# Attention and leaky-ReLU MLP on one core: the first two batches' values over 128 partitions, and a new order of the first loads

## The chip, the cores and the metric

The kernel runs on one core of one Trainium2 chip. The metric is the device time of one execution in microseconds (us), as the median of three runs. A lower time is better.

## The reference

The program is an attention over windows, followed by a two-layer MLP on its output. There are 8 batches, 8 heads, 576 rows and 64 columns per head; all inputs and the output are fp32.

```
scores = scale * np.matmul(q, k.transpose(0, 1, 3, 2))
rel = pos[:, None] - pos[None, :]
mask_plain = (rel >= 0) & (rel < 32)                         # heads 0 to 3
mask_dil = (rel >= 0) & (rel < 128) & (rel % 4 == 0)         # heads 4 to 7
attn = softmax of scores under the head's mask
attn_out = np.matmul(attn, v)
x = attn_out.transpose(0, 2, 1, 3).reshape(4608, 512)
h = x @ w_in                                                 # 512 x 2048
g = np.maximum(0.01 * h, h)
out = g @ w_out                                              # 2048 x 512
```

## The kernel before

**Visits.** Every batch is done in four visits of two heads each, in the order `VISITS = (2, 3, 0, 1)` (L434): first the two pairs of dilated heads ("group 1"), then the two pairs of plain heads ("group 0"). A pair's q and k, transposed, and its values lie in one of six slots of the tile `slots`; within a slot the keys begin at column `KB` and the values at `VB`.

**Batches 0 and 1** (`EARLY = 2`) use a form with 128 key rows of a head pair, of which the two heads own the even and the odd partitions. `unit` does half a visit: the scores on TensorE (L944), a bias of the mask added by a matmul (L941), the exponential on ScalarE (L951), the sums (L962) and the values (L956) on TensorE, logarithm and exponential on ScalarE for the reciprocal (L972, L974), and the normalised product on VectorE into the transposed activations `xt` (L985). `rest_unit` does the last 64 rows of all heads (the exponential of the reciprocal at L1055). In the scores' matmul both heads' keys stand in one operand: those of one head in 64 partitions at every second column, those of the other in the other 64 partitions at the columns between, and what is left must be zero. So the key part of every slot is cleared once (L550), and so are the two staging tiles `vst` of the values, since a load fills only every second partition there.

**The way in.** `load` (L529) issues a DMA, all of them on SP's queue but the first keys and the first constants (ScalarE's queue). q and k land in `stg` tiles, are cast to fp16 into `nat` (L544 on ScalarE, L545 on VectorE and GpSimd), are transposed on TensorE for batches 0 to 2 (`turn`, L808) and copied out of PSUM into the slot (L556 ScalarE, L557 VectorE). Key copies of batches 0 and 1 write every second column, one copy per head. For batches 3 and later VectorE transposes (L780, L787). `load_v` (L658) brings the values into `vst` and casts them into the slot. For batches 0 and 1 it issues ten DMAs of 64 partitions, every second one, and makes two casts of 128x576 per visit; for later batches it issues four DMAs per batch over 128 contiguous partitions (of pieces of 1 KB for the dilated heads, 256 bytes for the plain heads and the last rows), and casts them in parts of 64 partitions.

**Weights** come in 16 pieces, w0 to w15: w0 to w7 are `w_in` (piece n has the rows of visit `VISITS[n % 4]` and the columns of half n // 4), w8 to w15 are `w_out`. A piece lands in a tile that is free at the time (`gt`, `wst`, parts of `xt`) and is cast to fp16.

**Batches 2 to 7** use `burst`, which does one visit in quadrants of 64x64 (scores at L1146, exponential L1245, mask L1252, the reciprocal at L1204 and L1211, the product at L1228), and is set between the matmuls of the MLP.

**The MLP** goes over 12 chunks of 384 tokens. `up` and `up_pair` multiply by `w_in` (L1275, L1309) and apply the leaky ReLU on ScalarE while leaving PSUM (L1291); the chunk's result is a tile `gt`. Chunks 8 to 11 use a scheme of seven products for eight blocks (`ups7`: L1408 the products, L1420, L1427 and L1431 what is put together). `down` (L1488) and, in seven products, `group` (L1577, sums at L1563) multiply by `w_out`; the output is stored through `osb`.

**What sets the order.** All work is given as tasks with costs to a list scheduler (`_Plan`, L212), which passes forward and backward over it, and writes an order for each engine. The word list `FIRST` (L36) gives the order of the first loads: q, k, v and r (the last 64 rows of q and k) with the batch's digit and then the group's (v01 are the values of batch 0, group 1), w with the piece's number, c the rest of the constants. Two tables correct the plan by task number: `NUDGE` (L38) shifts a priority, `HAND` (L151) fixes an engine. Constants tune it: `SERVE` multiplies the planner's time for a load after the first ones, and `PLACE + PACE * k` (L1755) is the up step of which burst k stands ahead. Before the first up matmul TensorE runs idle matmuls on zeros (L1691, L1851).

## Time and profile before

| | |
|---|---|
| median of 3 runs | 297.22 us (296.24 to 298.74) |
| the profiled execution | 297.45 us |
| its span in the profile | 295.4 us |
| TensorE (PE) busy | 283.2 us, 96% of the span |
| VectorE (DVE) busy | 230.7 us, 78% |
| ScalarE (ACT) busy | 212.5 us, 72% |
| GpSimd (POOL) busy | 79.4 us, 27% |
| moved by DMA | 47.04 MB in 140235 packets |

The profile shows one execution. The time between the span and the execution's own time, 2.05 us, lies around the first and the last instruction. The times of instructions are counted from the start of the span. A row of a time list gives start and length in us, the engine, the line of the kernel, the operation with what it writes and reads, its size, and in brackets the idle time of the engine ahead of it with what ended it. A row of a group gives the busy time and the mean length in ns of one instruction, then the idle time ahead of them. PEld is TensorE's loading of weights, which runs beside its matmuls; SPq is SyncE's queue, on which the DMAs are issued.

### The profile page before, as it was taken

What the parts mean: (1) busy time and instruction counts of PE and PEld (TensorE: products, weight loads), DVE (VectorE), ACT (ScalarE), POOL (GpSimd) and SP (SyncE); (2) the same over time, 40 slices, a digit from 0 to 9 for tenths busy, and PEclk for the clock granted to TensorE, in tenths of its full rate; (3) what the DMA queues carried; (4) which work ended last, traced back from release to release, by engine and by line L of the source; (5) the groups of instructions that cost most, each with busy time, mean ns of one, the idle gap of its engine ahead of it and who ended that gap; (6) DMA issues with size and microseconds to landing.
All of it is one profiled execution on the core that took longest, in us unless ns stands there. A gap on an engine that the chain in (4) does not pass through costs nothing.

```text
span 295.4 us, 9622 instructions
## 1 busy us (share of the span) xinstructions
PE 283.2 (96%) x3981; PEld 221.2 (75%) x3981; DVE 230.7 (78%) x451; ACT 212.5 (72%) x438; POOL 79.4 (27%) x132
## 2 busy tenths in 40 slices
PE   6779999999999989999899999999999999999995
PEld 2556767687666867776567776777899999999984
DVE  6676686985999879865769678997878889678582
ACT  4976888399798986997977888666536776665721
POOL 4333242221671754454454461000000000000000
PEclk9999999999999999999999999999999999999999
DMA  7899998979799999998999991012202110121213
GB/s 248 237 301 403 340 351 292 357 160 171 143 216 227 154 225 191 202 176 195 170 220 196 168 252 40 0 40 73 73 0 74 37 38 2 36 73 38 71 69 111
DMA packets 140235, 47.04 MB, mean 159 GB/s; under 512 B 118944, under 2 KB 137632, under 8 KB 140192
## 3 DMA queue, kind: packets, MB, share of 16 engines
q1 hardware_dynamic: 139504, 45.81, 61.9%
q8 instruction: 31, 0.51, 0.7%
q10 hardware_dynamic: 688, 0.63, 0.6%
q14 instruction: 12, 0.10, 0.1%
HBM read 36.99 MB, written 9.44 MB: 157 GB/s over the span
## 4 chain that ended last, share of the span: by engine, by line
PE 68%; DMA 12%; ACT 7%; DVE 5%; SPq 4%; issue 2%; POOL 1%; ACTq 0%; DVEq 0%; POOLq 0%
PE psum L1577 27%; PE psum L1275 14%; PE psum L1408 13%; PE psum L1488 5%; SPq L529 4%; PE psum L1309 4%; PE psum L1146 3%; DMA gt<-in_moe_w_in_dram 3%; ACT gt L1291 2%; DMA out_dram<-osb 2%; DMA con<-consts 2%; DMA vst<-in_v_dram 2%; ACT slots L556 1%; DMA stg<-in_k_dram 1%; DMA stg<-in_q_dram 1%
## 5 line engine op out<-in xcount | busy, mean ns | idle before, releaser
L1275 PE MATMUL psum<-xt,w_in 128*128 128x384 f16 x448 | 86.0, 326 | 3.3 <-ACT gt L1291 2.1
L1577 PEld LDWEIGHTS <-gt 128*128 128x128 f16 x768 | 74.3, 98 | 12.1 <-DVE gt L1563 0.2
L1577 PE MATMUL psum<-w_out,gt 128*128 128x256 f16 x512 | 64.2, 273 | 0.0
L1291 ACT ACTIVATE gt<-psum 128x384 f16<-128x384 f32 x112 | 53.2, 494 | 14.3 <-PE psum L1275 13.3
L1275 PEld LDWEIGHTS <-w_in 128*128 128x128 f16 x448 | 41.8, 98 | 27.0 <-issue 4.2
L545 POOL CAST nat<-stg 128x576 f16<-128x576 f32 (+1 forms) x42 | 30.8, 754 | 47.0 <-DMA stg<-in_k_dram 17.1
L545 POOL CAST slots<-vst 64x256 f16<-64x256 f32 (+2 forms) x58 | 29.2, 520 | 31.0 <-DMA vst<-in_v_dram 20.6
L1427 DVE TENSOR_TENSOR vst<-psum,vst 128x384 f32<-128x384 f32 x48 | 25.8, 553 | 7.4 <-PE psum L1408 6.4
L1431 ACT ACTIVATE gt<-vst 128x384 f16<-128x384 f32 (+1 forms) x32 | 21.3, 683 | 11.1 <-DVE vst L1427 11.0
L1228 DVE TENSOR_TENSOR xt<-psum,rc 128x448 f16<-128x448 f32 (+2 forms) x53 | 20.4, 424 | 7.8 <-ACT rc L1211 6.6
L544 ACT CAST slots<-vst 64x448 f16<-64x448 f32 (+3 forms) x43 | 20.3, 482 | 3.3 <-DMA vst<-in_v_dram 2.6
L1606 ACT COPY stg<-psum 128x512 f32<-128x512 f32 (+1 forms) x22 | 11.8, 538 | 15.1 <-PE psum L1577 14.9
L1245 ACT ACTIVATE ee<-psum 128x896 f16<-128x896 f32 (+3 forms) x31 | 21.5, 707 | 1.4 <-PE psum L1146 1.4
L1408 PEld LDWEIGHTS <-w_in 128*128 128x128 f16 x256 | 21.9, 98 | 0.4
L1252 DVE TENSOR_TENSOR ee<-ee,con 128x768 f16<-128x768 f16 (+1 forms) x24 | 17.0, 707 | 6.4 <-ACT ee L1245 6.2
L557 DVE COPY slots<-psum 128x512 f16<-128x512 f16 (+3 forms) x33 | 15.4, 484 | 7.4 <-PE psum L808 5.6
L1408 PE MATMUL psum<-xt,w_in 128*128 128x192 f16 x192 | 21.1, 246 | 0.0
L1420 ACT COPY vst<-psum 128x384 f32<-128x384 f32 x32 | 15.0, 475 | 6.9 <-PE psum L1408 5.7
L787 DVE STREAM_TRANSPOSE slots<-nat 128x576 f16<-128x576 f16 (+2 forms) x30 | 15.9, 556 | 3.3 <-POOL nat L545 3.2
L1204 ACT ACTIVATE rc<-psum 128x576 f32<-128x576 f32 x24 | 15.6, 651 | 2.6 <-PE psum L1146 2.2
L1408 PEld LDWEIGHTS <-stg 128*128 128x128 f16 x192 | 16.7, 98 | 0.5
L780 DVE STREAM_TRANSPOSE slots<-nat 128x576 f16<-128x576 f16 x20 | 14.5, 757 | 2.9 <-POOL nat L545 2.8
(105 smaller groups left out, 483.3 us busy)
## 6 DMA issues: line engine op xcount, KB each, us to landing
out_dram<-osb SPq DMA_DIRECT2D x32, 256.0 KB, 2.5
stg<-in_q_dram SPq DMA_DIRECT2D x40, 144.0 KB, 4.0
stg<-in_k_dram SPq DMA_DIRECT2D x40, 144.0 KB, 3.5
vst<-in_v_dram SPq DMA_DIRECT2D x12, 288.0 KB, 5.1
gt<-in_moe_w_in_dram SPq DMA_DIRECT2D x6, 512.0 KB, 8.9
vst<-in_v_dram SPq DMA_DIRECT2D x6, 512.0 KB, 4.9
stg<-in_q_dram SPq DMA_DIRECT2D x5, 512.0 KB, 7.0
stg<-in_k_dram SPq DMA_DIRECT2D x5, 512.0 KB, 7.9
```

The lines of the kernel that those rows point to most:

```text
L544: return nc.scalar.copy(out=dst, in_=src)
L545: return ENG[e].tensor_copy(out=dst, in_=src)
L787: return add("DVE", dur, [c_qk[o]] + old, lambda e: nc.vector.transpose(slot(tn, dst, 0, 128, [1, n1 - n0]), na[:, o * S + n0:o * S + n1]) ...
L1228: lambda e, args=args: nc.vector.tensor_tensor(out=args[0], in0=args[1], in1=args[2], op=ALU.mult), prio)
L1245: lambda e, p=p, np=np, part=part: nc.scalar.activation(out=at(et, 0, 128, 448 * p, [448, np], [1, n]), in_=part, func=AF.Exp, scale=SCALE ...
L1252: lambda e: nc.vector.tensor_tensor(out=at(et, 0, 128, 0, [448, 2], [1, n]), in0=at(et, 0, 128, 0, [448, 2], [1, n]), in1=at(con, 0, 128, ...
L1275: nc.tensor.matmul(ht[:, 0:n], at(w_in, 0, 128, vi * DFF + j // 2 * 256 + j % 2, [2, 128]), at(xt[m % 2], 0, 128, vi * 1152 + x0 + x, [1, n]),
L1291: lambda e: nc.scalar.activation(out=gt[c % NG][:, j * n_c + x:j * n_c + x + n], in_=ht[:, 0:n], func=AF.Prelu, alpha=0.01),
L1408: nc.tensor.matmul(bk[:, n * i:n * i + n], w(v, 2 * z + i), x(v), start=first and i == 0 and v == 0, stop=i == 1 and v == 1, skip_group_ch ...
L1427: return add("DVE", 0.08 + 2 * n * 0.00104, deps, lambda e: nc.vector.tensor_tensor(out=dst, in0=over(bk), in1=dst, op=ALU.add), begin + w ...
L1431: t = add("ACT", dur, deps + gt_free.get(c - NG, []), lambda e: nc.scalar.activation(out=dst, in_=src, func=AF.Prelu, alpha=0.01), begin + ...
L1577: nc.tensor.matmul(bk[:, x:x + HN], tl[:, off + j * step:off + j * step + 128], rhs(j), start=first and x == 0 and j == 0, stop=j == HJ - ...
```

## The change

**Values of batches 0 and 1.** They are loaded as those of the later batches are: 128 contiguous partitions, four DMAs per batch instead of ten. The two heads of a pair now own the lower and the upper 64 partitions and no longer the even and the odd ones. With that go the bias and the pair table of the constants, and the key copies, which now write contiguous columns. A batch's values are cast by 20 instructions on 64 partitions (of 256, 64, 320 and 256 columns) where eight of 128x576 did it; for half of them the plan may choose GpSimd, VectorE or ScalarE, for the other half, which move data between the partition halves, VectorE or ScalarE.

**Clears.** The four clears of `vst` (128x1152 fp32) are gone; the value part of each slot is now cleared as well as the key part (12 clears of 128x576 instead of 6).

**Table load.** ScalarE loads its activation table ahead of its first computing instruction and not ahead of its first DMA issues.

**Plan.** w7 is loaded ahead of the first values, w0 ahead of w1, w9 ahead of q10, and the order of the last weights is new. `SERVE` goes from 1.0 to 1.1, `PLACE` from 21.0 to 20.5, `PACE` from 4.25 to 4.6. The planner counts 0.5 us for the issue of a DMA that doesn't lie on 64 partitions (0.65 before). `NUDGE` and `HAND` are replaced whole; `HAND` has some 190 entries now, 11 before.

**Counts.** The compiled rows go from 451 to 445 on VectorE, from 440 to 453 on ScalarE, from 132 to 149 on GpSimd and from 199 to 187 on SP. GpSimd has 8 more casts of q and k, 3 more of the last rows and 7 more of weights; VectorE has 7 fewer of q and k. Of the value casts of batches 0 and 1 VectorE has 16 with 256 or 320 columns and three with 64, ScalarE ten and three. TensorE's matmuls are the same, with two more idle ones.

```diff
-ROOM, LATE, LANDS, SERVE, FSERVE = 256, 1.06, 0.6, 1.0, 1.04
+ROOM = 256
+LATE = 1.06
+LANDS = 0.6
+SERVE = 1.1
+FSERVE = 1.04
...
-PLACE = 21.0
-PACE = 4.25
+PLACE = 20.5
+PACE = 4.6
...
-FIRST = ('q01 q00 r0 v01 v00 w1 w0 w7 w2 w6 w3 w4 q11 w5 q10 v11 w9 w8 '
-         'w10 w13 w11 r1 v10 w12 w14 w15 c ')
+FIRST = ('q01 q00 r0 w7 v01 v00 w0 w1 w2 w6 w3 w4 q11 w5 w9 q10 v11 w10 '
+         'w8 w13 w11 r1 v10 w15 w12 w14 c ')
 NUDGE = {
-    0: 8.35, 2: 2.35, 3: -23.12, 8: -0.87, 9: -27.76, 10: -0.24, 25: -101.0, 30: -2.6, 33: 0.12, 36:
...
+    0: 87.72, 2: -74.14, 3: 109.34, 4: -121.33, 5: -62.38, 6: 44.63, 7: 83.91, 8: -101.47, 9: 29.63,
...
 HAND = {
-    61: "POOL", 338: "DVE", 454: "DVE", 459: "DVE", 763: "ACT", 764: "ACT", 1013: "ACT", 1389:
...
+    3: "DVE", 4: "DVE", 5: "DVE", 6: "DVE", 8: "DVE", 11: "DVE", 12: "DVE", 13: "DVE", 26: "DVE",
...
-TURN_AT = ('st01t', 'sssft')
+TURN_AT = ('fgfgt', 't0tft')
...
-    key = np.arange(128)[:, None] // 2
+    key = np.arange(128)[:, None] % 64
...
-    pairs = np.arange(128)[:, None] % 2 == np.arange(128)[None, :] // 64
+    pairs = np.arange(128)[:, None] // 64 == np.arange(128)[None, :] // 64
...
-        t = plan.dma(queue, 0.65, (took(n, size) * FSERVE if prio < -1400 else took(n, size, True) * SERVE), deps,
+        t = plan.dma(queue, 0.65 if dst.ap[0][1] == 64 else 0.5, (took(n, size) * FSERVE if prio < -1400 else took(n, size, True) * SERVE), deps,
...
-                               prio + 0.01 * i, deps) for x in (KB,)]
+                               prio + 0.01 * i + 0.001 * x / VB, deps) for x in (KB, VB)]
...
-    t_blank = [[clear((("DVE", 1.24), ("POOL", 1.4)), x[:, VH * hh:VH * hh + VH], None, 0.0, -2001)
-                for hh in range(2)] for x in vst]
...
+        if g:
+            lv = [load(queue, at(vs, 0, 128, 0, [256, 4], [1, 256]),
+                       dram(v, base, [4 * D, 128], [HS, 4], [1, 256]), 512, 1024, v_old, prio),
+                  load(queue, at(vs, 0, 64, 1024, [D, 4], [1, D]),
+                       dram(v, base + 512 * D, [D, 64], [HS, 4], [1, D]), 256, 256, v_old, prio + 0.01)]
+        else:
+            lv = [load(queue, at(vs, 0, 128, 576 * j, [D, 9], [1, D]),
+                       dram(v, base + 2 * j * HS, [D, 128], [128 * D, 9], [1, D]),
+                       1152, 256, v_old, prio + 0.01 * j) for j in range(2)]
...
-            made = [cast(slot(tn, VB + D * hh, 0, 128, [128, 9], [1, D]),
-                         at(vs, 0, 128, VH * hh + j * S, [D, 9], [1, D]), S, lv[hh][j] + old, prio,
-                         ("POOL", "ACT"), 1.3)
-                    for hh in range(2)]
+            elif g:
+                parts = [(h, ab, VB + 512 * ab + 64 * h, [[128, 4], [1, D]], 512 * j + 256 * h, [[D, 4], [1, D]], 256, 0)
+                         for h in range(2) for ab in (h, 1 - h)]
+                parts += [(h, 0, VB + 1024 + 64 * h, [[1, D]], 1024 + 128 * j + 64 * h, [[1, D]], 64, 1) for h in range(2)]
+            else:
+                parts = [(h, (h + s) % 2, VB + 128 * s + 64 * h, [[256, 5 - s], [1, D]],
+                          576 * j + 64 * ((9 * h + s) // 2), [[D, 5 - s], [1, D]], 320 - 64 * s, j)
+                         for h in range(2) for s in range(2)]
+            for h, ab, x, xd, y, yd, n, i in parts:
+                made.append(cast(slot(tn, x, 64 * h, 64 * h + 64, *xd), at(vs, 64 * ab, 64 * ab + 64, y, *yd), n,
+                                 [lv[i]] + old, prio, SHIFT if h != ab else ("POOL",) if b >= EARLY else
+                                 ("POOL", "DVE", "ACT")))
...
--            p0, p1, x = 64 * hh, 64 * hh + 64, KB + hh
+            p0, p1, x = 64 * hh, 64 * hh + 64, KB + 64 * hh
...
-        nc.scalar.preload_act_table_set("natural_log_exp_and_others")
+            if t.eng == "ACT" and not t.service and not tables:
+                nc.scalar.preload_act_table_set("natural_log_exp_and_others")
+                tables = True
```

The order of instructions moves at three places that the prediction speaks of. The first is SP's queue at the start, from the last rows of the keys of batch 0 on (`vst_73` takes the dilated heads' values, `vst_74` the plain heads', `gt_82` and `wst_89` the first weights). Before:

```order
L529 DMA stg_68<-in_k_dram 64x8x64
L529 DMA vst_73<-in_v_dram 64x2x256 x4
L529 DMA vst_73<-in_v_dram 64x2x64 x2
L529 DMA vst_74<-in_v_dram 64x9x64 x4
L529 DMA gt_82<-in_moe_w_in_dram 128x1024 x2
L529 DMA wst_89<-in_moe_w_in_dram 128x1024
```

And now:

```order
L686 DMA stg_68<-in_k_dram 64x8x64
L686 DMA wst_89<-in_moe_w_in_dram 128x1024
L686 DMA vst_73<-in_v_dram 128x4x256
L686 DMA vst_73<-in_v_dram 64x4x64
L686 DMA vst_74<-in_v_dram 128x9x64 x2
L686 DMA gt_82<-in_moe_w_in_dram 128x1024 x3
```

One weights piece (w7, into `wst_89`) stands ahead of the values, and the other weights follow after four value loads and not after ten.

The second place is ScalarE in the attention of batch 0, from the second half of the first pair of units on (`ee` the exponentials, `rc` the reciprocals, `slots` the copies of transposed q and k from `psum` and the casts of values from `vst`). Before:

```order
L951 ACTIVATE ee<-psum 128x320
L556 COPY slots<-psum 64x512
L951 ACTIVATE ee<-psum 128x320
L556 COPY slots<-psum 64x2x64
L544 CAST slots<-vst_73 128x9x64 x2
L972 ACTIVATE rc<-psum 128x256
L544 CAST slots<-vst_74 128x9x64
L974 ACTIVATE rc<-rc 128x256
L951 ACTIVATE ee<-psum 128x416
L544 CAST slots<-vst_74 128x9x64
```

And now:

```order
L713 COPY slots<-psum 64x8x64
L1083 ACTIVATE ee<-psum 128x320 x2
L713 COPY slots<-psum 64x2x64
L1104 ACTIVATE rc<-psum 128x256
L713 COPY slots<-psum 64x2x64 x2
L713 COPY slots<-psum 64x8x64
L701 CAST slots<-vst_73 64x4x64 x2
L1106 ACTIVATE rc<-rc 128x256
L701 CAST slots<-vst_73 64x64 x2
L713 COPY slots<-psum 64x8x64
L701 CAST slots<-vst_74 64x4x64
L1083 ACTIVATE ee<-psum 128x416
```

Four casts of 128 partitions with 576 columns have become casts of 64 partitions with 256 or 64 columns, and more copies of keys and last rows stand between the exponentials.

The third place is ScalarE at the values of the last batch (`gt_81` is written by the leaky ReLU of chunk 6, `gt_82` by that of chunk 7). Before:

```order
L1291 ACTIVATE gt_81<-psum 128x384
L544 CAST slots<-vst_73 64x2x2x64 x3
L544 CAST slots<-vst_74 64x448 x2
L544 CAST slots<-vst_73 64x128
L1291 ACTIVATE gt_81<-psum 128x384
L544 CAST slots<-vst_74 64x448
```

And now:

```order
L701 CAST slots<-vst_73 64x2x2x64 x2
L1423 ACTIVATE gt_82<-psum 128x384
L701 CAST slots<-vst_73 64x2x2x64
L701 CAST slots<-vst_74 64x448 x2
L1738 COPY stg_68<-psum 128x512
```

The casts of the last batch's values stand among the activations of the next chunk.

More of the change, by code (lines that the diff above doesn't have):

```diff
@@ new lines, in load_v @@
+        vs = vst[vn]
+        if g:
[7 more added lines that the diff above has]
+                       1152, 256, v_old, prio + 0.01 * j) for j in range(2)]
@@ new lines, in load_v @@
+        for j in range(2):
+            vi = 2 * g + j
+            tn, (users, old) = slot_of[b, vi], slot_users[b, vi]
+            made = []
+            if b >= EARLY:
+                if g:
+                    parts = [(h, ab, VB + 256 * ab, [[D, 2], [128, 2], [1, D]], 512 * j + 128 * h, [[256, 2], [D, 2], [1, D]],
+                              256, 0) for h in range(2) for ab in (h, 1 - h)]
+                    parts += [(h, 0, VB + 512, [[1, 128]], 1024 + 128 * j, [[1, 128]], 128, 1) for h in range(2)]
@@ L688, in load_v @@
                                      lv[j:j + 1] + old, prio, ("POOL",)))
-                    for h in range(2):
-                        made.append(cast(slot(tn, VB + S + 128 * h, 64 * h, 64 * h + 64, [1, 448]),
-                                         at(vs, 64 - 64 * h, 128 - 64 * h, 576 * j + 128 * h, [1, 448]), 448,
-                                         lv[j:j + 1] + old, prio, SHIFT))
-                v_in[b, vi] = made
-                v_users += made
-            return
-        lv = []
```

83 lines of the change are left out of this document (34 added, 49 removed), and 349 rows, old and new, of the table NUDGE.

## The prediction

> **What bounds the kernel now.** I read the page's totals and its 40 slices first, then the chain of waits, then the table of stretches, then the instructions in order of time where a stretch is not full.
>
> ```profile
> PE 283.2 (96%) x3981; PEld 221.2 (75%) x3981; DVE 230.7 (78%) x451; ACT 212.5 (72%) x438; POOL 79.4 (27%) x132
> PE   6779999999999989999899999999999999999995
> DMA  7899998979799999998999991012202110121213
> PE 68%; DMA 12%; ACT 7%; DVE 5%; SPq 4%; issue 2%; POOL 1%; ACTq 0%; DVEq 0%; POOLq 0%
> ```
>
> TensorE is the bound: 96% of the span, and two thirds of the chain that ended last. Its matmuls are the same before and after, so the change can only win where TensorE waits. The slices show where: the first three, and a few eights and a bit in the middle. The DMA row stays high up to slice 24 and then falls to nearly nothing, so up to about 180 us the loads run near their limit beside TensorE. The stretches put sizes on it (columns: length, then busy us of PE, PEld, DVE, ACT, POOL, the clock, the DMA share and GB/s).
>
> ```profile
> 0.00:20.00 20.00, 14.50 (x137) 8.66 (x138) 14.15 (x28) 13.98 (x30) 7.42 (x16) 1.00 0.84 259
> 30.00:45.00 15.00, 14.39 (x153) 10.71 (x151) 10.78 (x24) 13.12 (x30) 6.03 (x8) 1.00 1.04 338
> 45.00:100.00 55.00, 54.98 (x885) 38.92 (x884) 47.32 (x103) 44.80 (x103) 21.52 (x37) 1.00 0.95 219
> 100.00:120.00 20.00, 19.22 (x327) 14.40 (x326) 17.40 (x32) 16.07 (x32) 10.64 (x17) 1.00 1.01 195
> 138.00:145.00 7.00, 5.77 (x152) 3.59 (x152) 3.54 (x8) 6.30 (x13) 4.91 (x8) 1.00 0.84 140
> 180.00:280.00 100.00, 99.76 (x1245) 89.08 (x1243) 82.75 (x152) 63.34 (x123) 0.00 (x0) 1.00 0.12 41
> ```
>
> From 45 to 100 us and from 180 to 280 us there is nothing to win. From 30 to 45 TensorE stands idle for 15.00 - 14.39 = 0.61 us, from 100 to 120 for 0.78, from 138 to 145 for 1.23. The rest is the start.
>
> ```profile
> 3.00:11.00 8.00, 5.84 (x45) 3.13 (x44) 4.69 (x9) 4.68 (x9) 2.24 (x4) 1.00 1.05 347
> 11.00:17.00 6.00, 4.59 (x56) 3.22 (x56) 5.12 (x13) 5.44 (x15) 2.71 (x4) 1.00 0.75 185
> 14.00:15.00 1.00, 0.82 (x8) 0.47 (x7) 0.91 (x4) 1.00 (x3) 0.44 (x1) 1.00 1.08 249
> 17.00:26.00 9.00, 7.89 (x101) 5.52 (x99) 5.92 (x16) 6.67 (x18) 1.74 (x2) 1.00 1.00 363
> 5.80 7.59 SPq L529 DMA_DIRECT2D vst<-in_v_dram  x10
> 13.43 1.10 SPq L529 DMA_DIRECT2D gt<-in_moe_w_in_dram  x2
> 26.19 0.43 DVE L545 CAST w_in<-gt 128x512 f16<-128x512 f32 x1 [0.47 <-DMA gt<-in_moe_w_in_dram]
> 26.53 0.45 DVE L985 TENSOR_TENSOR xt<-psum,rc 128x288 f16<-128x288 f32 x1
> 24.53 0.42 ACT L1055 ACTIVATE rc<-rc 128x256 f32<-128x256 f32 x1
> 27.39 2.94 ACT L1291 ACTIVATE gt<-psum 128x384 f16<-128x384 f32 x7 [2.44 <-PE psum L1275]
> ```
>
> Read these in order. The ten value loads keep SP's queue busy from 5.80 to 13.39, and the first weights are issued only at 13.43. In the six microseconds from 11 the DMA engines move 185 GB/s, against 347 before and 363 after: a hole. Downstream, VectorE waits at 26.19 for the piece w3, and the last wanted normalised output (26.53) stands behind that cast. ScalarE has finished batch 0's attention at 24.53 + 0.42 = 24.95 and then idles 2.44 us until the first whole column of the up projection is there. So at the start the weights come last, and ScalarE's attention chain is 2.4 us ahead of them.
>
> **The change part by part.**
>
> *Value loads, w7.* Ten issues at 7.59/10 = 0.76 us become four. With w7 put ahead at 1.10/2 = 0.55, the first weights of the row behind are issued at 5.80 + 0.55 + 4 x 0.76 = 9.4 instead of 13.43. What counts is the landing. The hole is 6 x (347 - 185) = 0.97 MB, or 2.8 us at 347 GB/s. Not all of it closes: the plain heads' values and the tails (0.655 MB) keep pieces of 256 bytes, and where such loads alone kept the engines full (14 to 15 us) they moved 249 GB/s: 0.655/0.249 - 0.655/0.347 = 0.74 us. So the weights up to w3 land about 2.8 - 0.7 = 2.1 us earlier. Bounds: 0 (the hole is the packets' own) and 2.8. w7's place costs the values about 0.52 MB / 0.347 = 1.5 us, which they get back by having no issue gaps.
>
> *Copies and casts on ScalarE.* Their prices:
>
> ```profile
> L544 ACT CAST slots<-vst 128x576 f16<-128x576 f32 x4 | 2.6, 667 | 0.0
> L544 ACT CAST slots<-vst 64x256 f16<-64x256 f32 x14 | 5.6, 402 | 0.9 <-DMA vst<-in_v_dram 0.6
> L544 ACT CAST slots<-vst 64x128 f16<-64x128 f32 x7 | 1.9, 295 | 0.4 <-DMA vst<-in_v_dram 0.3
> L556 ACT COPY slots<-psum 64x512 f16<-64x512 f16 x7 | 5.1, 727 | 2.0 <-PE psum L808 1.7 <-DVE slots L557 0.3
> L556 ACT COPY slots<-psum 128x512 f16<-128x512 f16 x6 | 3.3, 585 | 0.0
> L544 ACT CAST nat<-stg 128x512 f16<-128x512 f32 x4 | 2.4, 616 | 2.6 <-DMA stg<-in_q_dram 2.6
> ```
>
> Between its first key copy and the end of batch 0's attention ScalarE has now 4 value casts, 3 key copies, 1 query copy and 1 rest copy: 4 x 0.667 + 3 x 0.727 + 0.585 + 0.295 = 5.73 us (the rest copy taken at the 64x128 price). After: 4 value casts of 256 columns, 2 of 64, 6 key copies, 3 rest copies and a weight cast: 4 x 0.402 + 2 x 0.295 + 6 x 0.585 + 3 x 0.295 + 0.616 = 7.21 us. That is 1.5 us more. The trace has no key copy with unit stride: I take the whole-tile copy (0.585), which reads and writes as many columns in runs; with the old copy's 0.727 it would be 2.3 more, and a 64-column value cast can be no dearer than the 128-column one. VectorE and GpSimd are less full there (5.12 and 2.71 of 6 us), and VectorE hands key copies away for its ten value casts.
>
> So the dense up projection begins when the later of two things is there: the weights, 2.1 us earlier, or the attention, 24.95 + 1.5 = 26.4, against 27.39. The first would allow 25.3, the second 26.4. The second decides: **A = -1.0 us**, with bounds -2.4 (ScalarE's lead fully used) and +0.5 (dear copies, and the values 0.6 late).
>
> *Clears and the table load: nothing.* The four blanks of the staging tiles go, six more clears of the slots come.
>
> ```profile
> L550 DVE MEMSET vst<- 128x1152 f32 x3 | 3.1, 1018 | 1.4 <-PEq L1902 1.0 <-issue 0.4
> L550 DVE MEMSET slots<- 128x576 f32 x2 | 1.1, 538 | 0.1
> 7.53 0.61 PE L808 MATMUL psum<-con,nat 128*128 128x128 f16 x8 [1.39 <-DMA con<-consts]
> ...
> 15.96 0.30 PE L956 MATMUL psum<-ee,slots 128*128 128x96 f16 x4 [0.58 <-DVE slots L557]
> ```
>
> VectorE then clears eight times, 1.0 + 8 x 0.54 = 5.3 us, and casts the first queries at about 5.5 to 6. TensorE cannot use them before the constants land at 7.5, which hides all of this; without that cover it would be up to 2 us. (The last row is TensorE's first values, for the check at the end.) ScalarE's table load moves behind three DMA issues and still ends before its first cast.
>
> *Later batches.* SERVE 1.1 and PACE 4.6 (from 4.25) make the planner expect loads 10% longer and put one visit's attention every 4.6 up steps, 8% further apart. The stalls there have one pattern:
>
> ```profile
> 107.29 0.40 ACT L544 CAST slots<-vst 64x256 f16<-64x256 f32 x1 [0.65 <-DMA vst<-in_v_dram]
> 108.26 0.81 PE L1275 MATMUL psum<-xt,w_in 128*128 128x384 f16 x4 [0.78 <-ACT gt L1291]
> 138.60 0.56 ACT L544 CAST slots<-vst 64x448 f16<-64x448 f32 x1 [1.70 <-DMA vst<-in_v_dram]
> 139.73 0.81 PE L1275 MATMUL psum<-xt,w_in 128*128 128x384 f16 x4 [0.44 <-ACT gt L1291]
> 141.18 0.81 PE L1275 MATMUL psum<-xt,w_in 128*128 128x384 f16 x4 [0.64 <-ACT gt L1291]
> ```
>
> A value cast stands on ScalarE before its load has landed; the activations queue behind it; TensorE runs out of free banks. In the new order the last batch's value casts stand among the activations of the next chunk, so the same loads have about one chunk more time, and DMA (1.01 and 0.84 busy in these two stretches) and ScalarE have less to do per microsecond. These stalls with the small ones beside them are 0.78 + 1.23 = 2.0 us. I take three quarters, **C = -1.5**; bounds -2.0 and +1.0 (as large a stall as one of these at a new place, the loads of q and k being more mixed). From 30 to 45 us the weights no longer come just in time: half of the 0.61, **B = -0.3**, bounds 0 and -0.6.
>
> Sum: -1.0 - 0.3 - 1.5 = -2.8. The profiled execution took 297.45 (span 295.4, and 2.05 around it), so 294.65; the median of the runs is 297.22, which is 0.23 lower, so **294.4 us**, 0.9% faster. A difference under 1% (3.0 us) is about what a measurement of this kernel cannot tell from none.
>
> **The rivals.**
>
> *Slower: GpSimd and VectorE block each other.* GpSimd gets eight more q and k casts and seven more weight casts of batches 0 to 2, while VectorE gets the value casts. One meeting of that kind is in the trace (columns of a time list: min/median/max; the last row is a group of the stretch 5 to 30 us):
>
> ```profile
> L545 DVE CAST w_out<-gt x5: 408/419/830, 41.3 to 50.3; 128x512 f16<-128x512 f32 x5
> L545 POOL CAST w_out<-gt x1: 1825/1825/1825, 40.0 to 40.0; 128x512 f16<-128x512 f32 x1
> L545 POOL CAST w_out<-wst x1: 800/800/800, 41.8 to 41.8; 128x512 f16<-128x512 f32 x1
> ...
> L545 POOL CAST w_in<-gt 128x512 f16<-128x512 f32 x3 | 2.6, 870 | 8.1 <-DMA gt<-in_moe_w_in_dram 8.1
> ```
>
> Two casts that overlap cost VectorE 0.83 - 0.42 = 0.41 us and GpSimd 1.0. If all 16 value casts of 256 and 320 columns that VectorE has in the first two batches met one, that is 6.6 us on the path to the first outputs; less the 2.8 gained, 297.45 + 3.8 - 0.23 = 301.0. It decides from 7 meetings on (7 x 0.41 = 2.9). Against it: the weight casts of both engines at 20 to 28 us all ended in their usual 0.43 and 0.87. The Trainium skill ("SBUF — State Buffer", section "Who interferes with whom") has the rule: copies and casts on VectorE that use both ports and any GpSimd instruction hold the shared pair for the whole instruction, and the other blocks fully. By that rule such meetings are the norm for fp32 casts out of SBUF; the trace agrees with its 1.825 us, and shows it once in these casts. Chance 0.12.
>
> *No change.* ScalarE's copies at the dear price take the start's gain (2.3 of 2.44), and the late stalls come back elsewhere, since the same bytes must pass the same full DMA engines up to 180 us. For it: the DMA row. Against it: the casts' later places. 297.45 - 0.1 - 0.2 - 0.23 = 296.9. Here too belongs that the loads do not come earlier at all because the 256-byte pieces set their speed. Against that: a quarter of the DMA time from 11 to 17 was idle (0.75). Chance 0.22.
>
> *Clearly faster.* ScalarE's casts hide in its gaps, the start wins the whole 2.4, and the stalls of 30 to 45 and 100 to 145 all go: 2.4 + 0.6 + 2.0 = 5.0, so 292.2. For it: the weights' 2.1 nearly allows it. Against it: ScalarE was busy 5.44 of 6 us from 11 to 17. Chance 0.16.
>
> **How the numbers follow.** The forecast has 0.50, with its own range 292.4 to 296.4. The whole range, 291.0 to 298.8, takes in the clearly faster case and no change with a new stall of about 1.6 us, and leaves most of the slower case out. Faster by over 1% is below 294.2: 0.16 and half of the forecast's 0.50, 0.41. Slower by over 1% is above 300.2: 0.12. Within 1%: 0.47.
>
> **What would show it.** Right: first weights issued near 9.4 us; no DMA hole from 11 to 17 us (over 250 GB/s); VectorE waiting for no weights at 22 to 26 us; the first activation of the up projection near 26.4 or earlier with ScalarE's wait before it under 1 us; no value cast on ScalarE that waits over 0.5 us for its load after 100 us. Wrong: GpSimd casts of 1.2 us and more in the first 40 us with VectorE's value casts near 0.7; first values on TensorE clearly after 16 us (now 15.96); TensorE idle more than 2 us from 45 to 180 us; or a start that wins nothing though the weights come early, which would put the bound on ScalarE.

## The result, and the profile after

The changed kernel ran in 294.22 us (median), the kernel before beside it in 297.45: a ratio of 0.9896, with a 95% interval of 0.9854 to 0.9938. Run again, unchanged, it took 293.83 against 297.8: 0.9848 (0.9816 to 0.9881). So it is faster by 1.0 to 1.5%, 3 to 4 us. One execution of 579 us, nearly twice the others, is left out of the comparison.

The profiled execution of the changed kernel took 294.69 us, its span is 292.9. The page shows the following (totals, the slices of TensorE, of the DMA engines and of the granted clock, the shares of the chain that ended last).

```profile
PE 283.5 (97%) x3983; PEld 222.1 (76%) x3983; DVE 225.0 (77%) x445; ACT 214.4 (73%) x451; POOL 87.8 (30%) x149
PE   7879999999999999999999999999999999999995
DMA  7999999895999988799999888411212010112123
PEclk9979999999999999999999999999999999999999
PE 88%; ACT 4%; DVE 3%; DMA 2%; issue 1%; ACTq 0%; DVEq 0%
```

The eights in the middle of the TensorE row are gone. TensorE's share of the chain went from 68% to 88%, that of the DMA engines from 12% to 2%. One slice, the third, has a granted clock of 0.7: a spell at half clock, which two of the four executions had and two had not. I therefore read the times of the start in the profile of the second measurement, which has none (293.93 us, span 292.1). Its stretches, in the columns of the prediction's table:

```profile
0.00:30.00 30.00, 24.45 (x248) 15.69 (x249) 20.85 (x50) 21.82 (x54) 11.04 (x24) 1.00 0.97 323
11.00:17.00 6.00, 4.45 (x50) 3.03 (x50) 4.80 (x14) 5.78 (x19) 1.63 (x4) 1.00 1.05 277
30.00:45.00 15.00, 14.81 (x158) 11.11 (x156) 10.10 (x26) 13.48 (x36) 6.76 (x13) 1.00 1.02 330
45.00:100.00 55.00, 54.63 (x877) 38.23 (x875) 39.21 (x82) 45.98 (x106) 22.61 (x39) 1.00 0.92 210
100.00:180.00 80.00, 79.73 (x1315) 58.17 (x1314) 61.31 (x116) 66.11 (x129) 37.63 (x63) 1.00 0.90 177
180.00:200.00 20.00, 20.00 (x398) 15.22 (x396) 19.69 (x31) 16.59 (x33) 7.18 (x10) 1.00 0.33 95
```

And the three of these stretches that were not shown of the kernel before:

```profile
0.00:30.00 30.00, 23.92 (x244) 15.26 (x245) 20.05 (x44) 20.64 (x48) 10.90 (x20) 1.00 0.90 299
100.00:180.00 80.00, 77.93 (x1355) 56.55 (x1354) 61.49 (x114) 67.00 (x131) 40.96 (x68) 1.00 0.95 194
180.00:200.00 20.00, 19.76 (x333) 14.47 (x331) 19.33 (x32) 13.58 (x26) 0.00 (x0) 1.00 0.05 16
```

TensorE's idle time from 30 to 45 us went from 0.61 to 0.19, from 100 to 180 us from 2.07 to 0.27. In its place 0.37 is new from 45 to 100 us (0.02 before). After 180 us the DMA engines are now a third busy, where they had been nearly done (0.33 against 0.05): the loads are stretched out. The DMA hole at 11 us is filled (277 GB/s against 185).

Busy time does not say how far the work has come, since idle matmuls and waiting ones count too. For that I add up what is left after a given time: the columns of all of TensorE's matmuls that end after it, without the idle ones, over 2400 per us (a 384-column matmul takes 0.16 us where many follow each other: four last 0.81 us, eight 1.46, in rows below). The whole kernel is 292.05 us by this count.

| work left, us | after 30 us | after 100 us | after 280 us |
|---|---|---|---|
| before | 279.1 | 205.1 | 12.05 |
| changed (second measurement) | 279.3 | 205.1 | 8.85 |

At 30 us the changed kernel is 0.2 behind, at 100 us the two are even, with the same 1144 matmuls of the later batches' attention to come in both. The whole gain of 3.2 us is made between 100 and 280 us. The start won nothing.

The rows of time at the start, in the profile of the second measurement, show why. A row that joins several instructions gives the size of its first: among VectorE's six casts at 14.91 is one of 64x64.

```profile
5.92 6.28 SPq L686 DMA_DIRECT2D vst<-in_v_dram  x4
12.25 2.72 SPq L686 DMA_DIRECT2D gt<-in_moe_w_in_dram  x3
13.70 0.57 POOL L702 CAST slots<-vst 64x256 f16<-64x256 f32 x2 [0.81 <-DMA vst<-in_v_dram]
14.91 1.79 DVE L702 CAST slots<-vst 64x256 f16<-64x256 f32 x6
16.75 0.63 PE L1088 MATMUL psum<-ee,slots 128*128 128x96 f16 x8 [1.00 <-DVE slots L702]
25.55 0.42 DVE L702 CAST w_in<-gt 128x512 f16<-128x512 f32 x1
26.41 0.42 ACT L1187 ACTIVATE rc<-rc 128x256 f32<-128x256 f32 x1
27.45 1.64 ACT L1423 ACTIVATE gt<-psum 128x384 f16<-128x384 f32 x4 [0.63 <-DVE xt L1193]
```

Four value loads hold SP's queue for 6.28 us, hardly less than ten did (7.59). GpSimd gets the first values at 13.70, after waiting for them; before, that was 11.96:

```profile
11.96 1.43 POOL L545 CAST slots<-vst 128x576 f16<-128x576 f32 x2 [1.20 <-DMA vst<-in_v_dram]
```

VectorE casts six pieces in a row, and TensorE, which waits 1.00 us for the last of them, has its first values at 16.75 (15.96 before). On the other side the last weight cast ahead of the up projection, at 25.55, waits for no load any more. The attention of batch 0 is what comes last now: ScalarE ends it at 26.41 + 0.42 = 26.83, and the first activation follows at 27.45, against 27.39 before.

### The profile page after: what moved, and what is told of

It reads as the page before. It is cut to its first block, busy times and chain, and to the rows that moved or that the text cites. A ratio compares the mean times of both kernels' runs of the same rounds, so it can differ in the third digit from the quotient of the medians.

```text
span 292.9 us, 9624 instructions
## 1 busy us (share of the span) xinstructions
PE 283.5 (97%) x3983; PEld 222.1 (76%) x3983; DVE 225.0 (77%) x445; ACT 214.4 (73%) x451; POOL 87.8 (30%) x149
## 2 busy tenths in 40 slices
DMA packets 140043, 47.04 MB, mean 161 GB/s; under 512 B 118752, under 2 KB 137440, under 8 KB 140000
## 4 chain that ended last, share of the span: by engine, by line
PE 88%; ACT 4%; DVE 3%; DMA 2%; issue 1%; ACTq 0%; DVEq 0%
PE psum L1709 32%; PE psum L1407 24%; PE psum L1540 13%; PE psum L1278 6%; PE psum L1620 5%; PE psum L1441 3%; DMA con<-consts 2%; PE psum L940 1%; DVE slots L702 1%; ACT slots L713 1%; PE psum L1094 1%; PE psum L1088 1%; DVE xt L1117 1%; PE psum L1073 1%; DVE slots L714 1%
## 5 line engine op out<-in xcount | busy, mean ns | idle before, releaser
L702 POOL CAST nat<-stg 128x576 f16<-128x576 f32 (+1 forms) x50 | 33.5, 693 | 43.5 <-DVE gt L1695 21.3
L702 POOL CAST slots<-vst 64x256 f16<-64x256 f32 (+4 forms) x56 | 27.0, 496 | 24.9 <-DMA vst<-in_v_dram 13.9
L701 ACT CAST slots<-vst 64x256 f16<-64x256 f32 (+4 forms) x54 | 22.5, 429 | 1.0
L1552 ACT COPY vst<-psum 128x384 f32<-128x384 f32 x29 | 13.6, 475 | 11.7 <-PE psum L1540 11.2
L714 DVE COPY slots<-psum 128x512 f16<-128x512 f16 (+3 forms) x22 | 10.3, 477 | 11.5 <-PE psum L940 4.3
L1384 DVE TENSOR_TENSOR ee<-ee,con 128x768 f16<-128x768 f16 (+1 forms) x24 | 14.4, 599 | 6.2 <-ACT ee L1377 6.1
L1746 DVE TENSOR_TENSOR osb<-psum,stg 128x512 f32<-128x512 f32 x21 | 14.3, 682 | 4.1 <-ACT stg L1738 2.3
L926 POOL COPY slots<-slots 128x512 f16<-128x512 f16 (+1 forms) x15 | 10.2, 690 | 23.7 <-DVE slots L919 17.2
L1738 ACT COPY stg<-psum 128x512 f32<-128x512 f32 (+1 forms) x18 | 9.9, 549 | 9.6 <-PE psum L1709 9.0
L1343 ACT ACTIVATE rc<-rc 128x576 f32<-128x576 f32 x24 | 16.6, 691 | 0.1
```

Of the source, the lines that this page charges most:

```text
L701: return nc.scalar.copy(out=dst, in_=src)
L702: return ENG[e].tensor_copy(out=dst, in_=src)
L1343: lambda e: nc.scalar.activation(out=rt, in_=rt, func=AF.Exp, scale=-1.0), prio)
```

## The experiments

Where tasks are moved by hand, the planner's finished order is taken, only the named tasks (the numbers) are given another place in it (a time on the plan's own scale), and the order is sorted anew. Each kernel is compared with the kernel before on the same chip. Three chips were used, on which the medians of before were 297.8 (23 runs, 296.27 to 301.36; the changed kernel once more, the layout alone, the late casts, w7 back), 297.87 (fewer bytes, the casts on GpSimd, the constants first) and 297.59 (the rest). Differences between two edited kernels by their medians can therefore hold a difference between chips.

### The changed kernel once more

No edit.

> The changed kernel once more, nothing edited. Its first profile had TensorE at half clock from 18 to 22 us. If that is chance, this profile shows a granted clock of 1.00 there, the first activation of the up projection well before 27.77 us (nearer 26.5), and a time of 293.7 to 294.3. If the dip belongs to the new start (more matmuls early), it is there again, at the same place, and the time is 294.2 to 294.7.

293.83 us (293.67 to 294.11), 0.9848 (0.9816 to 0.9881). Its profile is the one read above. These four runs differ by 0.44 us, where the 23 of before differ by 5; those of the first measurement differed by 0.94.

### The value layout alone, in the old order

The kernel before, with the loads, casts, key copies and clears of the change; first loads, constants and every other task at the engine and place that they had.

```diff
-        if b >= EARLY:
...
+        if g:
+            lv = [load(queue, at(vs, 0, 128, 0, [256, 4], [1, 256]),
...
+    for t, (eng, start, dur) in zip(plan.tasks, PLACED):
+        t.eng, t.start, t.dur = eng, start, dur
```

> The kernel before with the values of batches 0 and 1 over 128 partitions alone (four loads, the casts by halves, keys written contiguously, 12 clears); every other instruction keeps the place and the engine that it has before. Theory one (the weights came last at the start, and the loads of the values held them up): first weights issued near 11.2 us and not 13.43, the cast of w3 near 24.5 and not 26.19, 0.7 to 1.3 us faster than before, with the stalls at 108 and 139 us still there (0.78 and 1.1 us on TensorE). Rival (the start is set by the attention chain, and the whole gain comes from the new order later on): within 0.3 us of before.

297.1 us (294.49 to 299.59), 0.9962 (0.993 to 0.9994): about a third of a per cent faster, 0.7 to 1.1 us. The profiled execution, 295.26 us, is one of its quicker ones; its rows at the start:

```profile
4.96 4.79 SPq L860 DMA_DIRECT2D vst<-in_v_dram  x4
9.80 2.22 SPq L860 DMA_DIRECT2D gt<-in_moe_w_in_dram  x2
15.20 0.30 PE L1262 MATMUL psum<-ee,slots 128*128 128x96 f16 x4 [0.54 <-DVE slots L888]
24.43 0.42 ACT L1361 ACTIVATE rc<-rc 128x256 f32<-128x256 f32 x1
26.75 2.55 ACT L1597 ACTIVATE gt<-psum 128x384 f16<-128x384 f32 x6 [1.90 <-PE psum L1581]
...
106.81 0.81 PE L1581 MATMUL psum<-xt,w_in 128*128 128x384 f16 x4 [0.43 <-ACT gt L1597]
130.37 1.46 PE L1581 MATMUL psum<-xt,w_in 128*128 128x384 f16 x8 [0.52 <-ACT gt L1597]
```

With the values first, everything is early in this execution: the weights issued at 9.80, the first values on TensorE at 15.20, the first activation at 26.75. The work left after 100 us is 204.05, 1.1 less than before. So the layout does win about the microsecond that I had forecast for the start, and as the changed kernel has 205.1 left there, something else in the change gives it back. ScalarE still waits 1.90 us for the first column here, its attention having ended at 24.85; the weights are again what it waits for, the last of them being cast until 26.37. The stalls after 100 us stay, as they should: the old order of the later batches is untouched.

### The late value casts alone, in the old order

Six of ScalarE's value casts of the later batches in the kernel before, moved back behind four to six more of its activations.

```diff
+    MOVE = {736: 104.8, 742: 104.81, 740: 104.82, 916: 135.1, 915: 135.11, 919: 136.3}
+    for t in order:
+        t.start = MOVE.get(t.n, t.start)
```

> The kernel before with six value casts on ScalarE moved two to six activations later (those at 107.29, 108.23, 138.60, 139.70 and 141.15 us), nothing else edited. Theory one (the casts stood there before their loads, and the activations behind them held TensorE up): TensorE's waits at 108.26, 139.73 and 141.18 go (1.86 us together), 1.5 to 1.9 us faster than before. Rival (the full DMA engines are the limit, so the wait comes back at the casts' new place or behind them): less than 0.5 us faster.

298.23 us (296.35 to 300.24), 1.0003 (0.9974 to 1.0033): nothing. The moved casts, now at 109.31 and from 142.43 on, wait for no load any more. But two casts that were not moved, and had waited for nothing before, now do:

```profile
117.31 1.14 ACT L544 CAST slots<-vst 64x448 f16<-64x448 f32 x2 [1.18 <-DMA vst<-in_v_dram]
120.11 0.81 PE L1275 MATMUL psum<-xt,w_in 128*128 128x384 f16 x4 [0.61 <-ACT gt L1291]
...
127.65 0.83 ACT L544 CAST slots<-vst 64x256 f16<-64x256 f32 x2 [1.48 <-DMA vst<-in_v_dram]
128.91 0.81 PE L1275 MATMUL psum<-xt,w_in 128*128 128x384 f16 x4 [0.45 <-ACT gt L1291]
```

Each wait on ScalarE is still followed, within three us, by a wait of TensorE for an activation. The table of waits (total, count, longest) puts ScalarE's waits for value loads at 2.6 us in three before, and at 3.0 in three here. The loads of these two landed at 117.23 and 127.57, 0.3 and 1.3 us later than in the kernel before (116.93 and 126.27). So the wait that went at one cast came again at the next load; why these loads came later, this run does not show.

### Fewer bytes in the late loads, in both orders

In both kernels the plain heads' value loads of batches 3 to 7 bring two pieces of 64 columns per partition where nine belong, 2.3 MB less in all; the plan and its order stay. The seven pieces that are left out make the output wrong, so this is a test and no kernel to use.

```diff
-                lv = [load(queue, at(vs, 0, 128, 576 * j, [D, 9], [1, D]),
-                           dram(v, base + 2 * j * HS, [D, 128], [128 * D, 9], [1, D]),
+                lv = [load(queue, at(vs, 0, 128, 576 * j, [D, 2 if b > 2 else 9], [1, D]),
+                           dram(v, base + 2 * j * HS, [D, 128], [128 * D, 2 if b > 2 else 9], [1, D]),
```

> The kernel before with the loads of the plain heads' values of batches 3 to 7 cut to two of nine pieces (7/9 of 2.95 MB less; what isn't loaded stays as an earlier batch left it, so the output differs); every instruction and its order are the same. Theory one (from 100 to 180 us the loads run late because the DMA engines are full, and value casts on ScalarE, first copies of q and k on GpSimd and all behind them wait for bytes): TensorE's idle time from 100 to 180 us falls from 2.07 to under 0.7 us, 1.5 to 2.5 us faster than before, and its runs lie closer together. Rival (the order itself holds TensorE up there, whatever the loads do): under 0.5 us faster.

> The changed kernel with the same cut of loads (plain heads' values of batches 3 to 7, two of nine pieces; the output differs). Theory one (its order no longer waits for loads after 45 us): within 0.4 us of the changed kernel. Rival (loads still cost it something behind full engines): 0.6 to 1.5 us faster than the changed kernel.

The old order takes 295.77 us (295.13 to 297.56), 0.9937 (0.9913 to 0.996), 2.1 less than the full kernel before. The changed order takes 294.17 (293.59 to 296.29), 0.9891 (0.9852 to 0.993), no less than with all its bytes. The stretches from 100 to 180 us, of the old order and then of the changed one:

```profile
100.00:180.00 80.00, 79.13 (x1363) 57.31 (x1361) 63.07 (x116) 68.71 (x134) 38.73 (x67) 1.00 0.83 167
```

```profile
100.00:180.00 80.00, 79.73 (x1378) 58.26 (x1377) 59.78 (x114) 66.31 (x129) 40.15 (x65) 1.00 0.83 157
```

Fewer bytes take TensorE's idle time in the old order from 2.07 to 0.87 us, and in the table of waits ScalarE has none left for a value load. In the changed order it is 0.27 with all the bytes and 0.27 with fewer. So the stalls of the old order came from late loads, on DMA engines that were 0.95 busy in this stretch, and the changed order does not depend on them. The cut takes away bytes and the 256-byte packets that carry them; which of the two counts, it does not tell.

### w7 back behind the values

In the changed kernel w7 is loaded behind w4, and cast there.

```diff
+    MOVE = {40: 13.02, 42: 24.2, 41: 24.3}
+    for t in order:
+        t.start = MOVE.get(t.n, t.start)
```

> The changed kernel with w7 loaded behind w4 and not ahead of the values, its two casts behind those of w4; nothing else edited. Values and the first weights then come 512 KB earlier, 1.3 us at 380 GB/s. Theory one (in the changed kernel the start is set by the chain of attention over ScalarE, VectorE and TensorE): values land near 12.2 us and not 13.5, but the first activation of the up projection moves by less than 0.5 us, and the time by less than 0.4. Rival (loads still come last at the start): 1.0 to 1.3 us faster than the changed kernel.

295.49 us (294.29 to 296.3), 0.9899 (0.9869 to 0.993): not faster, rather 1.7 slower by the medians. Five of the six runs had a spell at half clock, though; the one without took 294.29, 0.5 above the changed kernel's median.

```profile
4.99 4.99 SPq L686 DMA_DIRECT2D vst<-in_v_dram  x4
11.46 0.59 POOL L702 CAST slots<-vst 64x256 f16<-64x256 f32 x2 [1.00 <-DMA vst<-in_v_dram]
15.22 2.45 DVE L702 CAST slots<-vst 64x256 f16<-64x256 f32 x6
15.77 0.61 POOL L702 CAST w_in<-gt 128x512 f16<-128x512 f32 x1 [1.56 <-DMA gt<-in_moe_w_in_dram]
17.27 0.30 PE L1088 MATMUL psum<-ee,slots 128*128 128x96 f16 x4 [1.21 <-DVE slots L702]
```

The values are there 2.2 us earlier (11.46 against 13.70), and it helps nobody, because VectorE has its six value casts no earlier in its order than before. They begin at 15.22, and they now meet a weight cast of GpSimd at 15.77 and take 2.45 us where they took 1.79. TensorE's first values come at 17.27, half a microsecond later, and before the spell begins. So w7's place alone is not what costs the start; its place and that of the casts go together.

### The same, with the early casts on GpSimd

As above, and seven of the value casts that stay in their half of the partitions go to GpSimd, as soon as the values land.

```diff
+    MOVE = {40: 13.02, 42: 24.2, 41: 24.3, 47: 12.52, 51: 12.53, 53: 12.54, 49: 12.55, 55: 12.56,
+            59: 14.3, 61: 14.31, 65: 15.67, 48: 11.47, 52: 11.48, 54: 11.49, 50: 11.5}
+    ON = dict.fromkeys((47, 51, 53, 49, 59, 61, 65), "POOL")
+    for t in order:
+        t.start, t.eng = MOVE.get(t.n, t.start), ON.get(t.n, t.eng)
```

> The changed kernel with the start rearranged, the rest of the order as it is: w7 and its casts behind w4, and of batch 0's value casts all that stay in their partition half (10) on GpSimd; VectorE casts four of the dilated heads in the gap that w7's cast leaves, ahead of the copies of the last rows. Theory one (the start is set by the chain of attention, and in it by VectorE's row of six value casts ahead of the first values): first values on TensorE at 15.0 to 15.6 us and not 16.3 to 16.75, the first activation of the up projection 0.7 to 1.2 us earlier than 27.45, 0.7 to 1.2 us faster than the changed kernel, no half clock at 18 to 22 us. Rival (GpSimd's casts of values and weights block VectorE's copies and casts, as they did with w7 alone moved): first values not before 16.3, same time or up to 1 us slower.

293.02 us (292.53 to 293.86), 0.9844 (0.9818 to 0.9869), by the medians 0.8 less than the changed kernel.

```profile
11.33 4.41 POOL L702 CAST slots<-vst 64x256 f16<-64x256 f32 x10 [1.10 <-DMA vst<-in_v_dram]
13.02 1.26 DVE L702 CAST slots<-vst 64x256 f16<-64x256 f32 x4
15.34 0.45 PE L1088 MATMUL psum<-ee,slots 128*128 128x96 f16 x8
26.19 1.64 ACT L1423 ACTIVATE gt<-psum 128x384 f16<-128x384 f32 x4 [0.63 <-DVE xt L1193]
```

TensorE's first values come at 15.34 without a wait, the first activation at 26.19, 1.26 earlier. Of this 0.9 is left at 100 us (work left 204.2 against 205.1).

### The constants first, and both together

ScalarE's queue brings the constants ahead of the first keys; once in the changed kernel, once with the edit above.

```diff
+    MOVE = {1: -0.01}
```

> The changed kernel with the constants issued ahead of the first two key loads on ScalarE's queue and not behind them; nothing else edited. Theory one (TensorE's first transposes wait for the constants, and the whole chain of attention starts there): first transposes near 6.1 us and not 6.9 (then the first casts bind), everything behind them 0.5 to 0.8 us earlier, 0.4 to 0.8 us faster than the changed kernel. Rival (the first keys come later by the 104 KB, 0.3 us, and the constants' landing was set by full engines and not by their place): no difference over 0.2 us.

> The changed kernel with both edits of the start: w7 behind w4 and the half-keeping value casts of batch 0 on GpSimd, and the constants issued ahead of the first keys. If the two gains stand on the same chain one behind the other, they add: 293.83 - 0.8 - 0.4 = 292.6 (292.2 to 293.0). If the earlier constants only bring the chain to another wait (the values, which land near 11.4 us, or VectorE's copies), the time is that of the first edit alone, 293.0.

The first alone takes 293.5 us (292.62 to 294.16), 0.9854 (0.9822 to 0.9886): 0.3 under the changed kernel by the medians, with runs that overlap (293.67 to 294.11), so that a gain of its own is not shown. Both together take 292.24 (292.1 to 292.42), 0.9829 (0.9794 to 0.9865). The intervals of the ratios carry the wide spread of the kernel before; the runs themselves do not overlap with the changed kernel's, six between 292.1 and 292.42 against 293.67 to 294.11, nor with those of the edit above (292.53 to 293.86). Both together is the best version found: 5.3 us under the kernel before and 1.6 under the changed one. Its rows:

```profile
15.00 0.45 PE L1088 MATMUL psum<-ee,slots 128*128 128x96 f16 x8
25.84 1.64 ACT L1423 ACTIVATE gt<-psum 128x384 f16<-128x384 f32 x4 [0.63 <-DVE xt L1193]
```

The first activation is 1.6 us earlier than in the changed kernel, and the end is 1.6 us earlier. After 100 us 203.5 are left, against 205.1. Here the start is the bound, and what it wins arrives at the end whole.

### Fewer idle matmuls

In the changed kernel TensorE runs no idle matmuls between 12 and 16 us of the plan's scale: seven fewer.

```diff
-        while t.start > 0.5 and x + 0.3 < u.start:
+        while t.start > 0.5 and x + 0.3 < u.start and not 12.0 < x < 16.0:
```

> The changed kernel without the seven idle matmuls that TensorE runs between the scores and the first values of batch 0 (from 13.9 to 17.2 us); nothing else edited, and TensorE has nothing else to do there. Theory one (TensorE drops to half clock for some 4 us when it has been too idle in the microseconds before): a granted clock of 0.994 or less in every run, and 0.5 to 1.5 us slower than the changed kernel. Rival (the half clock falls by chance, or from load): the clock is 1.00 in about half the runs as with the changed kernel, same time.

294.48 us (293.94 to 295.44), 0.9903 (0.9868 to 0.9937); the mean granted clock was 0.987 to 0.994 in all six runs. The stretches of 16 to 18 and 18 to 22 us, first here, then in the second measurement of the changed kernel:

```profile
16.00:18.00 2.00, 0.61 (x9) 0.45 (x10) 1.89 (x6) 1.81 (x6) 0.80 (x2) 1.00 0.96 371
18.00:22.00 4.00, 4.00 (x52) 3.58 (x52) 3.42 (x9) 3.63 (x11) 1.59 (x3) 0.57 0.96 331
```

```profile
16.00:18.00 2.00, 0.82 (x9) 0.48 (x10) 1.88 (x7) 1.92 (x6) 0.84 (x2) 1.00 0.94 342
18.00:22.00 4.00, 3.14 (x52) 2.51 (x52) 3.83 (x10) 3.85 (x12) 1.49 (x3) 1.00 0.96 340
```

After the idle stretch the granted clock is 0.57 on average over four microseconds, and 52 matmuls fill all of them, which at the full clock take 3.14 us. The price is 0.65 us by the medians, which come from two chips. It is the spell of the changed kernel's first profile, now in every run.

### Both kernels without their tables

`NUDGE` and `HAND` empty, everything else as it is.

```diff
+NUDGE = {}
+HAND = {}
```

> The kernel before with both tables by task number left empty, so that the planner's own order stands: the base for the run beside it. Slower than before by 1 to 8 us.

> The changed kernel with both tables by task number left empty. Theory one (SERVE 1.1 and PACE 4.6, with the new layout, make the planner leave the late loads more time, as the prediction said): 2 us or more faster than the kernel before with empty tables, and no value cast on ScalarE waits over 0.5 us for its load after 100 us. Rival (the tables hold the gain of the later stages): within 1 us of the kernel before with empty tables, or slower.

The old constants and layout without tables take 298.45 us (295.0 to 299.96), 1.0015 (0.9979 to 1.005), the new ones 293.96 (293.82 to 294.09), 0.9887 (0.9847 to 0.9927). The whole difference is there without either table. From the old kernel's profile the stretch and ScalarE's line in the table of waits, then the stretch of the new one:

```profile
100.00:180.00 80.00, 77.44 (x1346) 56.13 (x1344) 62.98 (x116) 63.08 (x126) 41.30 (x70) 0.99 0.92 189
```

```profile
ACT slots L430 <- DMA vst<-in_v_dram: 5.2, 5, 2.4
```

```profile
100.00:180.00 80.00, 80.00 (x1323) 58.72 (x1320) 57.79 (x109) 66.05 (x131) 37.42 (x62) 1.00 0.91 178
```

Under the old rules ScalarE waits 5.2 us for value loads and TensorE stands idle for 2.56; under the new ones TensorE is busy without a break, and ScalarE has no such line.

## Why the prediction was right in its sum and wrong in its parts

The sum holds: 294.4 us predicted, 294.22 measured, and -2.8 on the profiled execution's own time against -2.76 (297.45 to 294.69) and -3.5 in the profile without the half-clock spell. But that is luck: two terms missed on opposite sides, one by 1.2 us and the other by 1.7.

**A, the start: -1.0 predicted, +0.2 measured.** The branch was chosen rightly: the weights stopped being last, and the attention decides. Its time was wrong. The step that failed is "w7's place costs the values about 0.52 MB / 0.347 = 1.5 us, which they get back by having no issue gaps". They got 0.5 us back and not 1.5, and the price was higher: with w7 behind them, the values are there at 11.46, 0.5 us earlier than before, and with w7 ahead at 13.70, 2.2 us later than that. I had priced an issue at 0.76 us whatever it carries, so that four would take 3.0; they took 6.28 (5.75 in the first profile), the last alone 3.53 (3.00). The weights were issued at 12.25 and not at 9.4, the values were 1.7 us later than before (13.70 against 11.96), and not at most 0.6. VectorE's six casts ahead of the first values then made it 0.8 on TensorE. The price of ScalarE's copies, which I was less sure of, was right: a key copy in runs takes 0.578 us, taken at 0.585.

```profile
L713 ACT COPY slots<-psum 64x512 f16<-64x512 f16 x8 | 4.6, 578 | 2.4 <-PE psum L940 1.9 <-DVE slots L714 0.5
```

ScalarE ended batch 0's attention at 26.83, close to the 26.4 of the sum. But the sum took that end for the start of the up projection, and between the two stand VectorE's last products and the first column: 27.45 - 26.83 = 0.62 us that I left out. Before, this step had been hidden under the wait for the weights. With 0.43 from the later attention that is 1.05 of the miss of 1.2. The experiments close it from the other side: the layout alone wins 0.7 to 1.1 us, and the changed kernel with w7 back and the casts on GpSimd has its first activation at 26.19, nearly where the sum had put it.

**B, 30 to 45 us: -0.3 predicted, -0.4 measured** (TensorE's idle time from 0.61 to 0.19). Right. From 45 to 100 us, where the sum had nothing, the idle time grows by 0.35, and at 100 us the two kernels are even.

**C, the later batches: -1.5 predicted, about -3.2 measured** (the work left after 100 us is equal, after 280 us it is 3.2 less). The place and the sign were right, the size was half, and the reason held only in part. Its first part, "the last batch's value casts stand among the activations of the next chunk, so the same loads have about one chunk more time", is not borne out where it was tried alone: no gain, other casts waited in the moved ones' place. (They stood only four to six activations later; a whole chunk was not tried.) It was the loads that were late: taking 2.3 MB out of them won 2.1 us in the old order and nothing in the new. The second part, that DMA has "less to do per microsecond", is what the DMA row shows. The attention matmuls left after 180 us are 352 against 288, one visit more, and the last values are issued at 179.6 and not 173.3 us. With the visits further apart the DMA engines have the time from 180 to 200 us as well, in which they had been idle (0.05 busy, now 0.33), and less is asked of them from 100 to 180 (177 GB/s against 194). My own rival said that "the same bytes must pass the same full DMA engines up to 180 us"; that limit of 180 us was itself a choice of the plan, and `PACE` can move it, which I did not see. The tables are not the cause, since the gain is there without them. Which of the new constants carries it (`PACE`, `SERVE`, `PLACE`, `TURN_AT`, the order of the first loads) was not tried singly and stays open; the stretched loads speak for `PACE`. Open too is the last microsecond of C, by which the new order gains more than fewer bytes gave the old one.

**The rival of blocked engines.** It exists, and it is small. In the changed kernel no cast on GpSimd took the 1.2 us that I had named as its sign (0.86 is the longest of the first 40 us), and the weight casts on GpSimd even became shorter (0.61 us where I had read 0.87 as usual):

```profile
L702 POOL CAST w_in<-wst 128x512 f16<-128x512 f32 x3 | 1.8, 613 | 2.6 <-DMA wst<-in_moe_w_in_dram 2.6
```

The 0.87 was already the price of a meeting. Before, each weight cast on GpSimd at 20 to 28 us began within 0.03 us of one on VectorE, as here, where GpSimd came second and lost 0.26 us, VectorE nothing:

```profile
20.06 0.43 DVE L545 CAST w_in<-gt 128x512 f16<-128x512 f32 x1 [0.34 <-DMA gt<-in_moe_w_in_dram]
20.09 0.87 POOL L545 CAST w_in<-gt 128x512 f16<-128x512 f32 x1 [4.25 <-DMA gt<-in_moe_w_in_dram]
```

Where VectorE comes second, it is VectorE that loses. With w7 back, one of its six casts began 0.05 us after GpSimd's weight cast (15.77 to 16.38) and ended 0.14 us after it:

```profile
15.82 0.70 DVE L702 CAST slots<-vst 64x256 f16<-64x256 f32 x1
```

It took 0.70 us where four of the others took 0.29; the sixth, at 17.05, met the next weight cast in the same way. This bears on the rule of the Trainium skill ("SBUF — State Buffer", section "Who interferes with whom"), by which, when a cast on VectorE uses both ports, the engine that comes first holds the shared ports for its whole instruction and the other waits. The trace agrees with it in the second case; in the first, GpSimd lost 0.26 of the 0.40 us that VectorE's cast still had to run. So meetings were there before the change too, and the prediction had taken their price for the usual time. But their price on the chain is small: the six casts lost 2.45 - 1.79 = 0.66 us, and where ten value casts on GpSimd ran beside VectorE's, the first values still came 1.4 us earlier (15.34). Both are far from the 6.6 us of the rival.

**The other points.** "No change" and "clearly faster" did not come. The clears and the table load cost nothing that the trace shows: TensorE's first transposes wait for the constants in both kernels. What would show each step was met for the DMA hole (277 GB/s), for the weights that nobody waits for, and for ScalarE's casts after 100 us (no wait for a load); it was missed for the issue time and the first activation. Two of the signs of being wrong came: the first values clearly after 16 us (16.75), and a start that wins nothing though the weights come early.

## What to carry to other kernels

Where casts wait for loads on full DMA engines, moving the casts back by a few instructions can leave the wait to the next load; spread the loads over the time in which the engine is idle, and test it by taking bytes out of the loads, which costs one run per order. When a wait goes, add up what the next thing in line still has to do after its own end, down to the first instruction of the bound engine: what the old wait hid is part of the new path. And a load set ahead of another on one queue is worth what the later one's users can lose: change the load's place and its users' places together, or the earlier data lie and wait.

## What the runs showed of the hardware

**Four issues took nearly as long as ten.** The values of batch 0, 1.18 MB, held SP's queue for 7.59 us in ten issues. In four they held it for 6.28 us with w7 ahead of them, for 4.76 with w7 back and the casts on GpSimd, and for 5.54 with the constants first as well. In the last two the issues began at 4.99 and at 4.23 us, and ended at 9.75 and 9.77 all the same. So the time is no fixed price per issue; what holds the queue, these runs do not show. The packets of the whole kernel stayed nearly the same (140235 and 140043).

**A spell at half clock lasts 3.41 us and follows a quiet stretch.** The 14 profiles show six spells with a granted clock of 0.50 ahead of the last matmuls, each 3.41 us long. The table has TensorE's busy time in the 3.41 us just ahead of each:

| kernel | spell begins, us | TensorE busy before it, us of 3.41 |
|---|---|---|
| changed, first profile | 18.82 | 1.71 |
| w7 back | 18.64 | 1.66 |
| fewer idle matmuls | 18.28 | 0.89 |
| changed, fewer bytes | 9.50 | 1.75 |
| the same | 19.74 | 1.48 |
| before, without tables | 177.73 | 1.36 |

None of these stretches was idle throughout: the longest single gaps that end in them last 0.80 (ahead of 19.74) to 2.06 us (ahead of 177.73). A quiet stretch alone does not decide it. The second measurement of the changed kernel has 3.41 us with only 1.64 busy (from 14.95 on), and with the constants first it is 1.74 (from 14.80 on), and both keep the full clock. What else decides, these runs do not tell. In the kernel before, the quietest 3.41 us between 9 and 26 us are 2.04 busy, with w7 back and the casts on GpSimd 1.85. So the change has brought its start closer to the spell, and the idle matmuls of this kernel earn their place.
